# A DeltaNet layer joined to a feed-forward block: the query-key product taken into the product of the keys with the state

## The chip, the cores and the metric

The kernel runs on one core of a Trainium2 chip. The metric is the device time of one execution in microseconds (us). Three runs of the kernel before gave 632.78, 633.17 and 633.45 us; their median, 633.17 us, is the time before. One further execution was recorded by the hardware profiler. In the profile, PE is the matrix engine (TensorE), PEld its weight loads, DVE the vector engine, ACT the scalar engine, POOL the GpSimd engine and SP the queue that issues most of the transfers. All data is float32.

## The reference: what is computed

There are 4 batches of 8 heads, 768 tokens and head size 48. Each of the 32 sequences keeps a 48 x 48 state. A token first reads the state with its query, and then corrects it with its key and value. The 8 heads of a token, 384 numbers, then go through a layer of 2048 with an exact GELU and back to 384.

```python
def _attn_ref(q, k, v, beta):
    k_n = k / (np.linalg.norm(k, axis=-1, keepdims=True) + 1e-06)
    state = np.zeros((B, H, D, D))
    for t in range(S):
        y[:, :, t] = einsum('bhd,bhde->bhe', q[:, :, t], state)
        v_old = einsum('bhde,bhd->bhe', state, k_n[:, :, t])
        state = state + beta * einsum('bhd,bhe->bhde', k_n[:, :, t], v - v_old)
def _moe_ref(x, w_in, w_out):          # x: 3072 x 384, the y of all tokens
    h = x @ w_in
    return (0.5 * h * (1.0 + erf(h / sqrt(2)))) @ w_out
```

## The kernel before, in words

**Chunks.** The 768 steps are cut into 12 chunks (c = 0 to 11) of C = 64 tokens. Inside a chunk the steps are turned into matrix products. A *unit* is a chunk of two batches with all 8 heads; `u.a` (0 or 1) tells which two, so every chunk has two units. The partitions hold two halves of 64 (`HALF`): for K, V and the results the half p is the batch. The state `St` (line 187) lies as 128 partitions x (unit, 2, 4, 48): the partition half r is the parity of the head, and the place in the third dimension is `p ^ r`, with p the batch and j (0 to 3) the pair of heads.

**The small matrix products.** The array of TensorE is used as four quadrants of 64 x 64. `QUADS` (line 48) names them in the order in which they are issued: (r, p) is the half of the partitions read, and the half written. One product over a unit is 4 pairs of heads x 4 quadrants = 16 matmuls; a float32 matmul shows as two records in the trace, so 32 records per unit.

**One chunk of the recurrence**, from chunk 2 on:

1. `against_state` (line 709): for each unit the transposed keys `Kt` times the state, 16 matmuls with 48 moving columns, and the transposed queries `Qt` times the state, 16 more. Both go into one PSUM tile `psK`.
2. `subtract` (line 731): DVE forms `psK - V` (L738) for each unit, then multiplies by the factor gm (L744); this is the right side of the solve. ACT copies the query part to `y` (L739).
3. `solve` (line 751): the triangular inverse `Zf` times that right side (psU, L762). `solved` copies the result U with ACT (L770, L772).
4. `queries` (line 447, through `products`, line 416): Q K^T of both units, 32 matmuls (64 records) with 64 moving columns, line 423. DVE multiplies the result by the causal mask into `P` (L459); for chunks from 4 on this is put off to a moment of its own (`cover`).
5. `outputs`: P times U (psY, L792), K^T times U for the new state (L803), then DVE adds to the state (L808) and forms the chunk's output (L818, with y).
6. `turns`: the output is transposed for the feed-forward block (L854).

Transposes of K and Q: for chunks 0 to 3 by TensorE (`transposed`, L402, copied by L403); from chunk 4 on by DVE in blocks of 32 x 32 (`turned_k`, L408, and `turned_q`, L413) out of `Kb` and `Qb`, which `load_blocks` (L138) fills by 8 transfers per unit. `Qt` is a tile with two buffers.

**PSUM.** The products of the recurrence share the pool tag `dn` (line 72), two buffers of two banks each, taken in turn. A product that starts a new `dn` tile waits until the tile before the last one has been read.

**The rest of TensorE's stream** is the feed-forward block: from chunk 4 on two chunks are worked at a time (`ffn_steps`), by a scheme with seven products for eight, in full-array matmuls of 256 columns (L994) and 192 columns (L928). They are tied in a fixed row (`behind`, line 935). Its sums and GELUs are on DVE and ACT (L1022 to L1107). Where a pair of heads' inverse is found, POOL eliminates row by row (L523, L525), after POOL's power (L360) and DVE's factors (L307 to L311).

**The order.** All steps carry a time `t` in units of a chunk of the feed-forward block, and `emit` writes them in that order. DVE runs in exactly that order (`manual_schedule`). The order on the other engines is chosen by the framework's scheduler when the kernel is built, save that `together` (line 610) ties the TensorE instructions of its steps into one unbroken row, and `keep` holds some ACT instructions in the order written. SP's transfers are issued in order, and a transfer whose target is still in use holds up those behind it. Each even chunk c from 4 on has its plan in the loop `for w in range(4, NC, 2)`: `begins` are the moments of join 1, join 2, then `against_state`, `solve`, `outputs`, `turns` of chunk w, and the last four those of chunk w+1.

Q K^T stands, before, at: chunk 2 alone (t = 2.725); chunks 3, 7, 9, 11 tied behind their solve; chunks 6, 8, 10 tied behind join 1; chunks 4 and 5 in steps of their own.

Of the kernel before, what the change touches and what calls it, by code (L numbers as in the profile page):

```python
# [8 lines left out]
F32 = mybir.dt.float32  # L9
# [5 lines left out]
ALU = mybir.AluOpType  # L15
# [4 lines left out]
def kernel(  # L20
# [82 lines left out]
    for c in range(NC):  # L103
        for a in range(NA):
# [6 lines left out]
            else:  # L111
                u.Kn, u.Kp = Kp[2 + a], Kp[(4 if c % 2 == 0 else 0) + a]
                u.Kb, u.Qb = blocks_of[a], blocks_of[2 + a]

    def load(c):
        for a in range(NA):
            u = tiles[c, a]
            fetch_in(u.Kp[:, :, 0:D], k, u)
            fetch_in(u.Qp[:, :, 0:D], q, u)

    def load_k(c, name):

# [176 lines left out]
    def heads(ap):  # L299
        return ap.rearrange("q (j r) d -> q r j d", r=2)  # L300
# [87 lines left out]
    def transposed(u, part=(0, 1)):  # L388
        for x in part:
            if x == 0:  # L390
                dst = u.Kt = wk.tile([128, 2, NP, C], F32, tag="Kt", name="Kt", bufs=6)
            elif u.c == 1:
                dst = u.Qt = su.tile([128, 2, NP, C], F32, tag="Qt1", name="Qt1")
            else:
                dst = u.Qt = wk.tile([128, 2, NP, C], F32, tag="Qt", name="Qt")
            if x and u.c == 3:
                psT = dn("psT")[:, 0].rearrange("q (j n) -> q j n", n=128)
            else:
                psT = sq("psT", NP, 128)
            flat = (Qp[2 + u.a] if u.c == 3 and x == 0 else (u.Kp, u.Qp)[x]).rearrange("q h d -> q (h d)")  # L400
            for j in range(NP):
                nc.tensor.transpose(psT[:, j, :], flat[:, j * 128:(j + 1) * 128], ident)  # L402
            nc.scalar.copy(dst.rearrange("q p j n -> q j p n"),  # L403
                           psT.rearrange("q j (p n) -> q j p n", p=2))
# [41 lines left out]
    def queries(us):  # L446
        c = us[0].c
        psP = products(us, 1)
        if c not in Ps:
            Ps[c] = (su if c == 1 else wk).tile([128, NA * H, C], F32, tag=f"P{c == 1}", name="P",  # L450
                                                bufs=1)
        for u in us:
            u.P = Ps[c][:, u.a * H:(u.a + 1) * H]
        dst = heads(Ps[c][:, us[0].a * H:(us[-1].a + 1) * H])
        if c < 2:
            nc.scalar.copy(dst, psP)
        else:
            both = mask.unsqueeze(1).to_broadcast([128, len(us) * H, C])
            masks[c] = lambda: nc.vector.tensor_tensor(dst, psP, heads(both), op=ALU.mult)  # L459
            if c < 4:  # L460
                masks[c]()

    masks = {}

    def cover(c):
        masks[c]()

    def masked(u, engine=nc.gpsimd):
        engine.tensor_tensor(u.P, u.P, mask_h, op=ALU.mult)
# [241 lines left out]
    def against_state(us):  # L711

        for u in us:
            u.W = u.V
            u.y = None
            if u.c == 0:
                nc.gpsimd.tensor_tensor(u.W, u.V,
                                        ng[:, u.a].unsqueeze(2).to_broadcast([128, H, D]),
                                        op=ALU.mult)
                continue  # L720
            u.psK = dn("psK")[:, :, 0:2 * NP * D].rearrange("q r (x j d) -> q x r j d", x=2, d=D)
            for x in range(2):
                for j in range(NP):
                    for r, p in QUADS:
                        rows = slice(r * C, r * C + D)
                        to = HALF[p ^ (j % 2)] if x and u.c > 1 else HALF[p]
                        nc.tensor.matmul(u.psK[to, x, r, j, :], lhsT=(u.Qt if x else u.Kt)[rows, p, j, :],  # L727
                                         rhs=St[rows, u.a, p ^ r, j, :], start=True, stop=True)
        if us[0].c > 2:
            subtract(us)  # L730

    def subtract(us):

        for u in us:
            if u.c == 0:
                continue
            u.y = wk.tile([128, H, D], F32, tag="y", name="y")
            nc.vector.tensor_tensor(heads(u.W), u.psK[:, 0], heads(u.V), op=ALU.subtract)  # L738
            nc.scalar.copy(heads(u.y), u.psK[:, 1])  # L739
        for u in us:  # L740
            if u.c == 0:
                continue
            gm = gms[u.c // 2][:, u.t]
            nc.vector.tensor_tensor(u.W, u.W, gm.unsqueeze(2).to_broadcast([128, H, D]),  # L744
                                    op=ALU.mult)

    def quarters(ap):

        return ap.rearrange("q p (k r d) -> q p k r d", r=2, d=D)

    def solve(us, copies=(nc.scalar.copy, nc.scalar.copy)):
        psU = dn("psU")
        for u in us:
            zf = Zf[(u.c // 2) % 2]
# [442 lines left out]
                sum_of_squares(*x)  # L1197
        queries([u])
    for a in range(NA):
        fetch_in(tiles[2, a].Qp[:, :, 0:D], q, tiles[2, a])  # L1200
    for a in range(NA):
        fetch_in(Qp[2 + a][:, :, 0:D], k, tiles[3, a])
    for n in range(2, NS):
# [66 lines left out]
    def state_at(c, *times, first=(), second=(), last=()):  # L1270

        steps = state_steps(c, first, second, last)
        if len(times) > len(steps):
# [11 lines left out]
    plan += [at(1.48, 1.8, sums), at(1.81, 1.811, [(1.0, fn, c) for c in (2, 3) for fn in (norms, prep)]), at(1.9, 1.905, [(1.0, finish_both)]), at(2.725, 2.726, [(1.0, queries, third)]),  # L1285
             at(1.31, 1.311, [(1.0, together, (against_state, first[NA:]))]),
             at(1.325, 1.326, [(1.0, subtract, first[NA:])]),
             at(1.42, 1.421, [(1.0, together, (solve, first[NA:], ()))]),
# [23 lines left out]
    for c in range(4, NC):  # L1312
# [15 lines left out]
    def query(c):  # L1328
        return [(queries, [tiles[c, a] for a in range(NA)])]

    def spread(name, n, *times):
        return [at(t, t + 0.001, [(1.0, copy_out, name, n)]) for t in times]
# [15 lines left out]
    for c in (2, 3, *range(4, NC, 2)):  # L1348
# [8 lines left out]
        else:  # L1357
# [7 lines left out]
             state_at(3, 3.367, 3.59, 3.72, 3.93, second=query(3))]  # L1365
    plan += rows_of(2, 3, ((1, 0.112, 0.113), (2, 0.14, 0.18), (31, 0.2, 0.6),
                           (1, 1.15, 1.151), (1, 1.155, 1.156), (1, 1.157, 1.158)))
    for w in range(4, NC, 2):
        more_to_come = w + 2 < NC
        if w == 4:  # L1370
            begins = 0.21, 0.29, 0.36, 0.45, 0.53, 0.63, 0.7, 0.77, 0.86, 0.93
# [11 lines left out]
        if w == 4:  # L1383
            one = [tiles[w, a] for a in range(NA)]
            plan += [[(t, (together, step)) for t, step in (
                (begins[0], (join_both, 2, 0)), (w + 0.235, *query(w)), (begins[1], (join_both, 2, 1)),
                (w + 0.335, *gram(w + 2)), (begins[2], (against_state, one[:1])),
                (w + 0.405, (against_state, one[1:])), (w + 0.49, *gram(w + 3)))],
                     state_at(w, None, *begins[3:6], last=query(w + 1))]
        else:  # L1390
            plan += [at(begins[0], begins[0] + 0.001, [(1.0, together, (join_both, w // 2, 0), *query(w))]),
                     at(begins[1], begins[1] + 0.001, [(1.0, together, (join_both, w // 2, 1), *gram(w + 2))]),
                     state_at(w, *begins[2:6], second=gram(w + 3))]
        plan += [state_at(w + 1, *begins[6:], second=() if w == 4 else query(w + 1))]
        plan += [at(w + t, w + t + 0.001, [(1.0, take, i % 2)]) for i, t in enumerate(takes)]
        plan += [at(t, t + 0.001, [(1.0, cover, c)])
                 for t, c in ((w + 0.24 if w == 4 else w - 0.261, w), (w + 0.64 if w == 4 else begins[7] + 0.03, w + 1))]
# [39 lines left out]
```

## Time and profile before

| what | value |
|---|---|
| median of 3 runs | 633.17 us (632.78 to 633.45) |
| the profiled execution | 634.08 us; its span 632.4 us; mean granted TensorE clock 0.982 |
| PE, PEld, DVE, ACT, POOL busy | 611.8, 546.6, 428.4, 241.5, 210.2 us |
| psG from Qt and Kt (L423) | 768 records in all, 640 of them in chunks 2 to 11; 48x64 |
| psK from Kt, and from Qt (L727) | 704 records each; 48x48 |
| mask P (L459) | 10 on DVE, 1214 ns each, 128x1024 |
| L738, L744 on DVE | 22 each, 552 and 576 ns, 128x384 |
| y (L739) on ACT | 22, 479 ns each |
| Q's transpose on DVE (L413) | 16, 687 ns each |
| transfers of Q's blocks on SP (L138) | 128; some 0.45 us each on the queue, 2.2 to 2.3 us to landing |

Busy time by stage, in us of the profiled execution:

| stretch | length | PE | DVE | ACT | POOL |
|---|---|---|---|---|---|
| 0 to 60 | 60 | 46.33 | 52.02 | 33.83 | 21.61 |
| 60 to 140 | 80 | 78.36 | 73.61 | 49.12 | 4.18 |
| 140 to 200 | 60 | 59.91 | 44.98 | 28.08 | 28.08 |
| 200 to 250 | 50 | 49.00 | 38.71 | 20.14 | 23.80 |
| 250 to 340 | 90 | 90.00 | 60.56 | 31.72 | 43.61 |
| 340 to 432 | 92 | 91.97 | 60.52 | 31.34 | 46.04 |
| 432 to 524 | 92 | 92.00 | 58.72 | 24.95 | 42.90 |
| 524 to 632 | 108 | 104.23 | 39.32 | 22.32 | 0.00 |

How to read it: the end of a matmul in the trace is modelled and successive matmuls overlap, so the time that a block takes from the stream is read from its start to the start of the next block, not from its busy time. Chunks 2 to 5 run at about 140, 184, 234 and 259 us; from there a pair of chunks takes about 92 us, with the even chunk's `against_state` at about 317, 409 and 500 us, and the odd one's 24 us later.

### The profile page before, as it was taken

To read this page: it belongs to the slowest core of one execution; us is meant where nothing else is said; L and a number is where in the kernel's file an instruction comes from. 1 tells how busy PE (TensorE), PEld (TensorE's weight loads), DVE (VectorE), ACT (ScalarE), POOL (GpSimd) and SP (SyncE) were. 2 spreads that over 40 slices of the span, in tenths; PEclk is the share of its full clock that TensorE was granted. 3 is DMA by queue.
4 is the path that set the end of the run, shared out by engine and by line. 5 is a ranking of instruction groups with operands and counts; after the bars stand their busy time and mean duration, and the time that the engine had idled before them with its cause. 6 is when DMAs were issued, how large, how long until landed. Compare 5 with 4: busy or idle time off the path is not lost.

```text
span 632.4 us, 20834 instructions
## 1 busy us (share of the span) xinstructions
PE 611.8 (97%) x8998; PEld 546.6 (86%) x8998; DVE 428.4 (68%) x783; ACT 241.5 (38%) x546; POOL 210.2 (33%) x316
## 2 busy tenths in 40 slices
PE   6779999999999999999999999999999999999997
PEld 5668886676899998998899998899998899988997
DVE  6999989999866597564868654967645955432532
ACT  3576876625452246224442024442024322044200
POOL 4045001000389721797112688113687100000000
PEclk9975999999999999999999999999999999999999
DMA  9794766102434433533024523025121001010011
GB/s 133 172 286 131 160 143 173 25 1 43 75 46 72 70 60 42 90 77 43 11 39 70 98 51 46 7 40 90 28 50 22 8 2 27 2 26 1 0 26 26
DMA packets 158428, 39.71 MB, mean 63 GB/s; under 512 B 150016, under 2 KB 153216, under 8 KB 158336
## 3 DMA queue, kind: packets, MB, share of 16 engines
q1 hardware_dynamic: 155664, 37.34, 31.0%
q10 hardware_dynamic: 2672, 1.03, 0.8%
q8 instruction: 71, 1.16, 0.8%
q14 instruction: 21, 0.17, 0.1%
HBM read 33.62 MB, written 4.72 MB: 61 GB/s over the span
## 4 chain that ended last, share of the span: by engine, by line
PE 76%; DVE 15%; DMA 3%; issue 2%; SPq 2%; ACT 1%; DVEq 0%
PE psX L928 12%; PE psY L994 10%; PE psY L928 9%; PE psX L994 8%; PE psV L994 5%; PE psZ L994 5%; PE psV L928 4%; PE psZ L928 4%; PE psK L727 3%; DVE Nu L525 3%; DVE tmp L523 3%; PE psO L895 3%; PE psG L423 2%; PE psH L877 2%; PE psY L792 2%
## 5 line engine op out<-in xcount | busy, mean ns | idle before, releaser
L360 POOL TENSOR_TENSOR n<-n,half 128x16 f32<-128x16 f32 x10 | 30.0, 3001 | 186.5 <-DVE n L358 136.6
L525 POOL TENSOR_TENSOR Nu<-Nu,tmp 128x30 f32<-128x30 f32 (+14 forms) x120 | 65.2, 543 | 9.0
L523 POOL TENSOR_TENSOR tmp<-Nu 128x30 f32<-128x30 f32 (+14 forms) x120 | 62.0, 517 | 9.3
L994 PE MATMUL psX<-xT,w_in_sb 128*128 128x256 f32 (+1 forms) x288 | 62.5, 346 | 0.0
L928 PE MATMUL psX<-w_out_sb,G 128*128 128x192 f32 x320 | 56.4, 329 | 0.0
L928 PEld LDWEIGHTS psX<-w_out_sb,G 128*128 128x128 f32 x320 | 52.1, 190 | 0.7
L994 PEld LDWEIGHTS psX<-xT,w_in_sb 128*128 128x128 f32 x288 | 47.9, 191 | 5.2
L877 PE MATMUL psH<-xT,w_in_sb 128*128 128x256 f32 x192 | 46.1, 396 | 0.8 <-ACT G L883 0.6
L877 PEld LDWEIGHTS psH<-xT,w_in_sb 128*128 128x128 f32 x192 | 37.1, 197 | 8.3 <-ACT G L883 1.9
L895 PE MATMUL psO<-w_out_sb,G 128*128 128x384 f32 x128 | 43.9, 490 | 0.0
L994 PE MATMUL psY<-xT,w_in_sb 128*128 128x256 f32 (+1 forms) x192 | 41.6, 346 | 0.0
L1022 DVE TENSOR_TENSOR psY<-psY,pu 128x512 f32<-128x512 f32 x20 | 14.0, 700 | 39.6 <-PE psY L994 38.8
L977 ACT COPY xT<-psX 128x768 f32<-128x768 f32 x9 | 7.2, 799 | 86.2 <-PE psX L854 86.2
L977 ACT COPY pu<-psZ 128x512 f32<-128x512 f32 x40 | 23.5, 587 | 35.2 <-PE psZ L994 35.2
L895 PEld LDWEIGHTS psO<-w_out_sb,G 128*128 128x128 f32 x128 | 23.6, 190 | 14.0
L994 PEld LDWEIGHTS psY<-xT,w_in_sb 128*128 128x128 f32 x192 | 32.1, 191 | 3.5
L977 ACT ACTIVATE G<-G 128x512 f32<-128x512 f32 x40 | 25.2, 630 | 19.2 <-DVE G L1030 19.1
L977 ACT ACTIVATE G<-psY 128x512 f32<-128x512 f32 x20 | 11.9, 597 | 44.7 <-PE psY L994 44.7
L1030 DVE TENSOR_TENSOR G<-psY,pu 128x512 f32<-128x512 f32 x20 | 13.7, 684 | 21.8 <-PE psY L994 21.7
L928 PE MATMUL psZ<-T,pu 128*128 128x192 f32 x160 | 28.3, 329 | 0.1
L928 PE MATMUL psY<-T,G 128*128 128x192 f32 x160 | 28.2, 329 | 0.0
L928 PE MATMUL psY<-w_out_sb,G 128*128 128x192 f32 x160 | 28.1, 329 | 0.0
(198 smaller groups left out, 1372.7 us busy)
## 6 DMA issues: line engine op xcount, KB each, us to landing
Kp<-in_k_dram SPq DMA_DIRECT2D x76, 96.0 KB, 3.4
w_out_sb<-in_moe_w_in_dram SPq DMA_DIRECT2D x24, 256.0 KB, 4.8
w_raw<-in_moe_w_out_dram SPq DMA_DIRECT2D x16, 384.0 KB, 5.0
V<-in_v_dram SPq DMA_DIRECT2D x48, 96.0 KB, 3.2
out_dram<-o_sb SPq DMA_DIRECT2D x40, 96.0 KB, 2.2
Qp<-in_k_dram SPq DMA_DIRECT2D x64, 32.0 KB, 2.4
Qp<-in_q_dram SPq DMA_DIRECT2D x64, 32.0 KB, 2.3
Qp<-in_q_dram SPq DMA_DIRECT2D x16, 96.0 KB, 4.6
```

Of the source, the lines that this page charges most:

```text
L360: nc.gpsimd.tensor_tensor(flat, flat, half, op=ALU.pow)
L423: nc.tensor.matmul(psG[HALF[p], r, i * NP + j, :], lhsT=u.Kt[rows, p, j, :], rhs=(u.Qt if x else u.Kt)[rows, p, j, :], start=True, stop=True)
L523: rows_on.tensor_tensor(tmp, nu[:, j + 1:, j:j + 1].to_broadcast([128, n, j]), nu[:, j:j + 1, 0:j].to_broadcast([128, n, j]), op=ALU.mult)
L525: rows_on.tensor_tensor(nu[:, j + 1:, 0:j], nu[:, j + 1:, 0:j], tmp, op=ALU.add)
L727: nc.tensor.matmul(u.psK[to, x, r, j, :], lhsT=(u.Qt if x else u.Kt)[rows, p, j, :], rhs=St[rows, u.a, p ^ r, j, :], start=True, stop=True)
L877: nc.tensor.matmul(psH, lhsT=w_in_sb[:, f // 2, m, f % 2 * 128:(f % 2 + 1) * 128], rhs=xTs[c][:, m, :], start=(m == 0), stop=(m == NM - 1))
L895: nc.tensor.matmul(u.psO, lhsT=G[:, u.a, f, :], rhs=w_out_sb[:, f, :], start=(f == 0), stop=(f == NF - 1))
L928: nc.tensor.matmul(ps_, lhsT=lhs[:, f, :], rhs=rhs[:, f, :], start=first and f == 0, stop=f == FH - 1, skip_group_check=not first)
L977: i = fn(*args, **kw)
L994: nc.tensor.matmul(ps_[:, i], lhsT=lhs[:, f // 2, f % 2 * 128:(f % 2 + 1) * 128], rhs=rhs, start=first and i == 0, stop=True, skip_group_c ...
L1022: nc.vector.tensor_tensor(L1["Y1"], L1["Y1"], L1["pu"][:, 0], op=ALU.add)
L1030: nc.vector.tensor_tensor(half(1, 1), shaped(L1["Y1"]), shaped(L1["pu"][:, 0]), op=ALU.add)
```

## The change

From chunk 2 on, the transposed queries are written beside the state, into one tile `SQ` of 48 + 64 = 112 columns per place. The product of the keys with it gives K times the state and K Q^T in the same 16 matmuls per unit; `queries` is no longer called for these chunks, and the mask into P is done by DVE from `psK` in `subtract`. The queries' product with the state becomes a function of its own, `against_queries`, placed at the head of `solve`, with a `dn` tile of its own for both units (`psQ`); the copies to y go with it. Since the place of a state in `SQ` is `p ^ r`, the queries of odd heads have to be loaded with the two batches changed over, so the transfers for r = 1 are split by batch (`fetch_q`, `load_blocks`). There is only one place for the transposed queries of a unit, where the tile before had two buffers; the times of `turned_q` for odd chunks are later (chunk 5: 4.57 for 4.4; chunks 7, 9, 11: c - 0.77 for c - 0.93). Chunks 0 and 1 keep their separate product.

```diff
+    def fetch_q(u):
+        rows = slice(u.c * C, (u.c + 1) * C)
+        for p in range(2):
+            for r in range(2):
+                nc.sync.dma_start(out=u.Qp[HALF[p ^ r], r::2, 0:D],
+                                  in_=q[2 * u.a + p, r::2, rows, :].rearrange("h t d -> t h d"))
...
                         to = slice((2 * r + e) * HB, (2 * r + e + 1) * HB)
+                        if r and name == "Qb":
+                            for p in range(2):
+                                n0_ = (2 * a + p) * H
+                                nc.sync.dma_start(
+                                    out=dst[to, 1 - p, :, h, 0:w],
+                                    in_=src[n0_ + 1:n0_ + H:2, rows,
+                                            e * HB:e * HB + w].rearrange("n t d -> t n d"))
+                            continue
...
-    St = cpool.tile([128, NA, 2, NP, D], F32)
+    SQ = cpool.tile([128, NA, 2, NP, D + C], F32, name="SQ")
+    St = SQ[:, :, :, :, 0:D]
...
     def turned_q(u):
-        u.Qt = wk.tile([128, 2, NP, C], F32, tag="Qt", name="Qt")
-        nc.vector.transpose(u.Qt.rearrange("q p j n -> q (p j n)"),
-                            u.Qb.rearrange("q p j h n -> q (p j h n)"))
+        u.Qt = SQ[:, u.a, :, :, D:]
+        nc.vector.transpose(u.Qt.rearrange("q p j n -> q (p j) n"),
+                            u.Qb.rearrange("q p j h n -> q (p j) (h n)"))
...
     def against_state(us):
...
-            u.psK = dn("psK")[:, :, 0:2 * NP * D].rearrange("q r (x j d) -> q x r j d", x=2, d=D)
-            for x in range(2):
-                for j in range(NP):
-                    for r, p in QUADS:
-                        rows = slice(r * C, r * C + D)
-                        to = HALF[p ^ (j % 2)] if x and u.c > 1 else HALF[p]
-                        nc.tensor.matmul(u.psK[to, x, r, j, :], lhsT=(u.Qt if x else u.Kt)[rows, p, j, :],
-                                         rhs=St[rows, u.a, p ^ r, j, :], start=True, stop=True)
+            w = D if u.c == 1 else D + C
+            psK = dn("psK")
+            u.psK = psK[:, :, 0:NP * w].rearrange("q r (j d) -> q r j d", d=w)
+            for j in range(NP):
+                for r, p in QUADS:
+                    rows = slice(r * C, r * C + D)
+                    nc.tensor.matmul(u.psK[HALF[p], r, j, :], lhsT=u.Kt[rows, p, j, :],
+                                     rhs=SQ[rows, u.a, p ^ r, j, 0:w], start=True, stop=True)
...
+    def against_queries(us):
+        c = us[0].c
+        if c > 1:
+            psQ = dn("psQ")[:, :, 0:NA * NP * D].rearrange("q r (a j d) -> q a r j d", a=NA, d=D)
+        for u in us:
+            if c > 1:
+                u.psQ = psQ[:, u.a]
+            for j in range(NP):
+                for r, p in QUADS:
+                    rows = slice(r * C, r * C + D)
+                    to, x = (HALF[p ^ (j % 2)], p ^ r) if c > 1 else (HALF[p], p)
+                    nc.tensor.matmul(u.psQ[to, r, j, :], lhsT=u.Qt[rows, x, j, :],
+                                     rhs=St[rows, u.a, p ^ r, j, :], start=True, stop=True)
+        for u in us:
+            u.y = wk.tile([128, H, D], F32, tag="y", name="y")
+            nc.scalar.copy(heads(u.y), u.psQ)
...
     def subtract(us):
...
         for u in us:
-            nc.vector.tensor_tensor(heads(u.W), u.psK[:, 0], heads(u.V), op=ALU.subtract)
-            nc.scalar.copy(heads(u.y), u.psK[:, 1])
+            if c > 0:
+                nc.vector.tensor_tensor(heads(u.W), u.psK[:, :, :, 0:D], heads(u.V), op=ALU.subtract)
+            if c > 1:
+                u.P = Ps[c][:, u.a * H:(u.a + 1) * H]
+                nc.vector.tensor_tensor(heads(u.P), u.psK[:, :, :, D:], heads(mask_h), op=ALU.mult)
...
     def solve(us, copies=(nc.scalar.copy, nc.scalar.copy)):
+        if us[0].c > 1:
+            against_queries(us)
         psU = dn("psU")
...
-        t = {4: 3.88, 5: 4.4}.get(c, c - (0.47 if even else 0.93))
+        t = {4: 3.88, 5: 4.57}.get(c, c - (0.47 if even else 0.77))
         plan += [at(t, t + 0.01, [(1.0, turned_q, u) for u in us])]
```

The steps `query(c)` and `cover` are taken out of the plan, and one time of the plan for chunk 5 (0.7) becomes 0.67. In the order that the built kernel has, chunk 5's `against_state` then stands directly behind chunk 4's `turns`, one L928 product earlier than before.

More of the change, by code (lines that the diff above doesn't have):

```diff
@@ L118, in load @@
             fetch_in(u.Kp[:, :, 0:D], k, u)
-            fetch_in(u.Qp[:, :, 0:D], q, u)
+            fetch_q(u)
     def load_k(c, name):
@@ L394, in transposed @@
             else:
-                dst = u.Qt = wk.tile([128, 2, NP, C], F32, tag="Qt", name="Qt")
+                dst = u.Qt = SQ[:, u.a, :, :, D:]
             if x and u.c == 3:
@@ L449, in queries @@
         if c not in Ps:
-            Ps[c] = (su if c == 1 else wk).tile([128, NA * H, C], F32, tag=f"P{c == 1}", name="P",
+            Ps[c] = (su if c == 1 else wk).tile([128, NA * H, C], F32, tag=f"P{c == 1:d}", name="P",
                                                 bufs=1)
@@ L453, in queries @@
             u.P = Ps[c][:, u.a * H:(u.a + 1) * H]
[L454 to L466, printed above, removed]
+        nc.scalar.copy(heads(Ps[c][:, us[0].a * H:(us[-1].a + 1) * H]), psP)
     def masked(u, engine=nc.gpsimd):
@@ new lines, in against_state @@
+            psK = dn("psK")
[5 more added lines that the diff above has]
+                                     rhs=SQ[rows, u.a, p ^ r, j, 0:w], start=True, stop=True)
+            if u.c == 1:
+                u.psQ = psK[:, :, NP * D:2 * NP * D].rearrange("q r (j d) -> q r j d", d=D)
+                against_queries([u])
@@ L732, in subtract @@
     def subtract(us):
+        c = us[0].c
+        if c > 1 and c not in Ps:
+            Ps[c] = wk.tile([128, NA * H, C], F32, tag="P0", name="P", bufs=1)
         for u in us:
[L735 to L738, printed above, removed]
-            nc.scalar.copy(heads(u.y), u.psK[:, 1])
-        for u in us:
[L741 to L745, printed above, removed]
+            if c > 0:
[3 more added lines that the diff above has]
+                nc.vector.tensor_tensor(heads(u.P), u.psK[:, :, :, D:], heads(mask_h), op=ALU.mult)
@@ L747, in quarters @@
+        for u in us:
+            if c > 0:
+                gm = gms[c // 2][:, u.t]
+                nc.vector.tensor_tensor(u.W, u.W, gm.unsqueeze(2).to_broadcast([128, H, D]),
+                                        op=ALU.mult)
     def quarters(ap):
@@ L1199 @@
     for a in range(NA):
-        fetch_in(tiles[2, a].Qp[:, :, 0:D], q, tiles[2, a])
+        fetch_q(tiles[2, a])
     for a in range(NA):
@@ L1284 @@
     sums = [(1.0, sum_of_squares, tiles[3, a], h) for a in range(NA) for h in range(H)]
-    plan += [at(1.48, 1.8, sums), at(1.81, 1.811, [(1.0, fn, c) for c in (2, 3) for fn in (norms, prep)]), at(1.9, 1.905, [(1.0, finish_both)]), at(2.725, 2.726, [(1.0, queries, third)]),
+    plan += [at(1.48, 1.8, sums), at(1.81, 1.811, [(1.0, fn, c) for c in (2, 3) for fn in (norms, prep)]), at(1.9, 1.905, [(1.0, finish_both)]),
              at(1.31, 1.311, [(1.0, together, (against_state, first[NA:]))]),
@@ L1326, in gram @@
         return [(grams, [tiles[c, a] for a in range(NA)])] if c < NC else []
-    def query(c):
-        return [(queries, [tiles[c, a] for a in range(NA)])]
     def spread(name, n, *times):
@@ L1364 @@
              at(3.11, 3.111, [(1.0, finish, 4)]),
-             state_at(3, 3.367, 3.59, 3.72, 3.93, second=query(3))]
+             state_at(3, 3.367, 3.59, 3.72, 3.93)]
     plan += rows_of(2, 3, ((1, 0.112, 0.113), (2, 0.14, 0.18), (31, 0.2, 0.6),
@@ L1370 @@
         if w == 4:
-            begins = 0.21, 0.29, 0.36, 0.45, 0.53, 0.63, 0.7, 0.77, 0.86, 0.93
+            begins = 0.21, 0.29, 0.36, 0.45, 0.53, 0.63, 0.67, 0.77, 0.86, 0.93
             takes = 0.212, 0.214, 0.292, 0.294
@@ L1385 @@
             plan += [[(t, (together, step)) for t, step in (
-                (begins[0], (join_both, 2, 0)), (w + 0.235, *query(w)), (begins[1], (join_both, 2, 1)),
+                (begins[0], (join_both, 2, 0)), (begins[1], (join_both, 2, 1)),
                 (w + 0.335, *gram(w + 2)), (begins[2], (against_state, one[:1])),
                 (w + 0.405, (against_state, one[1:])), (w + 0.49, *gram(w + 3)))],
-                     state_at(w, None, *begins[3:6], last=query(w + 1))]
+                     state_at(w, None, *begins[3:6])]
         else:
-            plan += [at(begins[0], begins[0] + 0.001, [(1.0, together, (join_both, w // 2, 0), *query(w))]),
+            plan += [at(begins[0], begins[0] + 0.001, [(1.0, together, (join_both, w // 2, 0))]),
                      at(begins[1], begins[1] + 0.001, [(1.0, together, (join_both, w // 2, 1), *gram(w + 2))]),
                      state_at(w, *begins[2:6], second=gram(w + 3))]
-        plan += [state_at(w + 1, *begins[6:], second=() if w == 4 else query(w + 1))]
+        plan += [state_at(w + 1, *begins[6:], second=())]
         plan += [at(w + t, w + t + 0.001, [(1.0, take, i % 2)]) for i, t in enumerate(takes)]
-        plan += [at(t, t + 0.001, [(1.0, cover, c)])
-                 for t, c in ((w + 0.24 if w == 4 else w - 0.261, w), (w + 0.64 if w == 4 else begins[7] + 0.03, w + 1))]
         if more_to_come:
```

## The prediction

> **What bounds the kernel now.** I read the page's busy times and slices, then the stages, then the chain, then the instructions in order of time around one chunk. One part of the page, three of its lines:
>
> ```profile
> PE 611.8 (97%) x8998; PEld 546.6 (86%) x8998; DVE 428.4 (68%) x783; ACT 241.5 (38%) x546; POOL 210.2 (33%) x316
> ...
> PE   6779999999999999999999999999999999999997
> ...
> PE 76%; DVE 15%; DMA 3%; issue 2%; SPq 2%; ACT 1%; DVEq 0%
> ```
>
> TensorE is busy in every slice from about 50 us on, and the chain is TensorE for 76%. From 250 to 524 us its busy time equals the stretch: work taken off its stream there shortens the run, if nothing that it waits for gets late. The stream around chunk 9's recurrence (start, length, line, shapes, records):
>
> ```profile
> 432.31 0.68 PE L727 MATMUL psK<-St,Kt 48*64 48x48 f32 x32
> 432.81 0.65 PE L727 MATMUL psK<-St,Qt 48*64 48x48 f32 x32
> 433.27 0.65 PE L727 MATMUL psK<-St,Kt 48*64 48x48 f32 x32
> 433.74 0.65 PE L727 MATMUL psK<-St,Qt 48*64 48x48 f32 x32
> 434.32 2.87 PE L928 MATMUL psY<-w_out_sb,G 128*128 128x192 f32 x16
> 437.02 2.76 PE L928 MATMUL psV<-w_out_sb,G 128*128 128x192 f32 x16
> 439.71 1.15 PE L762 MATMUL psU<-V,Zf 64*64 64x48 f32 x64
> 440.68 1.13 PE L423 MATMUL psG<-Qt,Kt 48*64 48x64 f32 x64
> 441.74 2.87 PE L928 MATMUL psX<-w_out_sb,G 128*128 128x192 f32 x16
> ```
>
> Read the starts, not the lengths (they overlap). A float32 matmul leaves two records. 32 records of 48 columns take 433.27-432.81 = 0.467 us, 58.4 ns for four; the four quadrants of the array run at once. Starts of the 64-column block, counted in narrow windows, also come four in 58.4 ns. So 48 and 64 columns cost the same: a floor per instruction, which a longer moving operand could use up. The full array has no such floor: L994's 128x256 blocks start every 863 ns for four records, 215.8 each; 128x192 162.5; 128x128 109.2. These three lie on 0.833 ns per column plus 2.5 ns. A visit to small tiles costs 0.04 us more on entry and 0.11 on leaving, and the product ahead of it 0.1.
>
> VectorE between this chunk's product with the state and its solve:
>
> ```profile
> 433.54 0.56 DVE L738 TENSOR_TENSOR V<-psK,V 128x384 f32<-128x384 f32 x1 [0.61 <-PE psK L727]
> 434.47 0.56 DVE L738 TENSOR_TENSOR V<-psK,V 128x384 f32<-128x384 f32 x1 [0.38 <-PE psK L727]
> 434.94 1.02 DVE L744 TENSOR_TENSOR V<-V,gm 128x384 f32<-128x384 f32 x2
> ...
> 445.25 1.22 DVE L459 TENSOR_TENSOR P<-psG,mask 128x1024 f32<-128x1024 f32 x1
> ```
>
> The right side is ready at 435.96, the solve (psU) starts at 439.71: 3.7 us of cover. The mask L459 comes off the path, after the solve.
>
> **The change, part by part.** 1. Removed: the block of Q with K in chunks 2 to 11, 64 records, 16 groups x 58.4 = 0.93 us, with its ends 1.06 behind psU (440.68 to 441.74) and 1.09 behind a join (psJ). Behind psU the leaving cost of 0.11 passes to psU, so 0.95 goes.
> 2. Longer: K with the state, 16 groups of 48 columns per chunk (0.93) become 16 of 112. No row has 112 columns in a quadrant. Low end: 58.4 ns a group, if the floor covered 112 too. High end: the two quadrants that read the same partitions take turns, 2 x 95.8 = 191.6. I take 0.833 x 112 + 2.5 = 95.8: the full array never beats that, and the 64-column group (55.8 by the same line) already runs all four at 58.4, so the rows nearest in shape show no turns. 16 x 95.8 = 1.53, so +0.60.
> 3. Moved: Q with the state (0.93) leaves the burst and goes in front of the solve, +0.95 there and -0.93 here, with its PSUM buffer in the place of the removed block's.
> The work per chunk is then, behind a join (6, 8, 10; 2 alike): -1.09 + 0.60 + 0.02 = -0.47; behind psU (3, 7, 9, 11): -0.95 + 0.62 = -0.33; chunks 4 and 5, where the block stood alone between products and also cost its neighbour 0.1 or twice 0.1: -0.67 and -0.57. Sum: 4 x 0.47 + 4 x 0.33 + 1.24 = 4.44 us off the stream.
> 4. The mask moves between L738 and L744: two of 128x512 per chunk. Bounds by row: half of L459's 1214 ns = 0.61, or L1022's 128x512 with PSUM on both sides, 0.70. I take 0.65. VectorE in sum: +20 x 0.65 - 12.1 = +0.9 us, at 68%. On the path +1.3 us per chunk against 3.7 us of cover (odd) and, in even chunks, L744 ending at 412.74 against a solve at 416.82. Cover: two to five feed-forward products. Without it 1.3 x 10 = 13 us. Queued behind: L1042 and the L358 sums. L1042 would end at 414.6 at the latest, before ScalarE's Gelu on it (414.82). L358 feeds POOL's 2.91 us power and then L307, which VectorE waits at: some 1.3 us later, repaid by the missing L459 (1.22) right behind.
> 5. Q's transpose now writes the one place beside the state, so it must follow the last read of the old Q. In chunks 7, 9, 11 it comes behind L1066 (ends 429.92), +1.29 = 431.2, while psK wants 432.31: 1.1 us of slack. In chunk 5 the built order puts psK one product earlier and the transposes behind L493 (254.30): 255.6, against a wanted start of 254.8 with the first half ready at 255.0. Cost 0.25; bounds 0 to 0.8.
> 6. The y copies (479 ns each) go from L738's wait to just ahead of the solve's copies. In chunks 6 and 8 the gram block behind psU takes psQ's buffer and must wait for both: ScalarE has L1078 (0.32) and two squares (0.94) queued when psQ starts, so y ends some 0.1 + 1.26 + 0.94 - 0.1 = 2.2 us after that; the block is ready after psQ and psU, 0.04 + 0.93 + 0.97 = 1.95. Cost 0.25 twice; bounds 0 to 0.5 each.
> 7. Gains on waits: in chunk 3 psZ and psX of L928 start at 196.03 and 199.09 and psY at 202.04, 3.06 and 2.95 apart instead of 2.70, with L408 late because it waited until 195.70 for the removed block, and psY waited 0.19 on L459. In chunk 4 psK waited at 234.31, 0.56 in all, with L459 (228.68) in front on a VectorE that had no idle time. Together some -1.1, bounds 0 to -1.5. Against it: the built order now interleaves chunk 4's second join with psZ, two more changes of tile size, +0.25; chunk 2's solve, L744 later by 1.3, +0.1.
> Items 5 to 7 cancel: 0.25 + 0.5 + 0.35 - 1.1 = 0.0 (from -1.5 to +2.2).
> 8. DMAs: Q's blocks of r=1 and Q of chunks 2, 3 are split: 8 x 8 + 8 = 72 more issues at about 0.45 us on SP. SP had four sends of chunk 8 at 438.26 behind the 16 Q issues at 421.36; now 24 that wait for the transpose at 431: sends near 441 to 444, landed by 447, and o_sb is next written behind psY at 454. Ahead of the first weights four more issues: +2 us on loads landing near 36 to 38, decoded from about 49. Both hidden; uncovered the first would cost some 5 us once per pair of chunks.
>
> Sum: 634.08 (the profiled run: span 632.4 and 1.7 around it) - 4.4 = 629.6; the median of the runs shown, 633.17, is 0.9 lower: **628.7**. By the bounds of 5 to 7: 627.2 to 630.9.
>
> **The rivals.** (a) Long columns overlap worse. By the line above one 64-column record would need 55.8 ns and one of 48 columns 42.5; four of either take 58.4, so the array does 3.8 and 2.9 records' work at once. With the lesser of the two, a group of 112 takes 4 x 95.8 / 2.9 = 132 ns: 160 groups x 36 = +5.8, **634.5, slightly slower**. For it: no row has more than 64 columns in a quadrant; against: the longer of the two rows overlaps better, not worse. The Trainium skill, "TensorE: Matmul & The Clock Gate", Part 3 ("Measured speedup vs the span model"), speaks for it: four row tiles with 512 columns gained 3.07 of 4, which as an estimate by that page would be 125 ns a group and 633.4 us here; this trace's 3.8 at 64 columns is better than that, and no run here shows longer ones. (b) Quadrants on the same partitions take turns beyond 64 columns: 160 x 95.8 = +15.3, **644, slower**. It decides from 124 ns a group, where the 4.4 is used up. Against: at 64 columns turns would already give 107. (c) The mask ahead of the solve makes VectorE or ScalarE late: 1.3 us in the four chunks 2 to 5, where VectorE is fullest (38.7 of 50 us in 200:250), gives +5.2: 633.9; in all chunks 641. For it: no idle time at 225 to 241; against: 2.4 us of cover left elsewhere, and L459 gone. (d) Q's single place stalls psK in 5, 7, 9, 11 by 0.5: 630.7. Against: the 1.1 us above.
>
> **How the numbers follow.** Forecast as summed 0.70, (d) 0.08, (c) 0.11 (0.02 faster, 0.05 same, 0.04 slower), (a) 0.05 (0.02 same, 0.03 slower, as the overlap is nearer 3.1 or 2.9 of 4), (b) 0.06. 0.2% is 1.3 us, about what a measurement of this kernel tells from none. Faster 0.80, same 0.07, slower 0.13. The range for 8 in 10: low 626.8, just under the gains of 7 in full; high 632.6, which takes in (d) and the smaller half of (c) and leaves (a) and (b) out.
>
> **What would show it.** psK's 32 records of one unit spaced near 24 ns, 0.77 us; 14.6 would mean a floor, 31 no gain, 48 turns. No psG from Qt after chunk 1. The next product's start minus psK's first near 1.7 us (2.01 before). psU starting straight behind psQ, without a wait for the right side (L744's product); a gap there is (c). A psK waiting on the Q transpose is (d). A gram block waiting on y in chunks 6 and 8 shows item 6. I am wrong if psK's spacing is off, or if TensorE's busy share falls below 97%.

## The result, and the profile after

The changed kernel is slower: 639.33 us median (637.69 to 642.88, four executions) against 633.31 us for the kernel before (632.78 to 634.15). The ratio is 1.0101, 95% interval 1.0056 to 1.0147. The forecast was 628.7 us and faster.

The profiled execution took 637.69 us (span 636.0), 3.61 us more than that of before. Its busy times and slices, and the chain:

```profile
PE 608.2 (96%) x8358; PEld 542.4 (85%) x8358; DVE 426.8 (67%) x793; ACT 240.7 (38%) x546; POOL 209.4 (33%) x316
...
PE   6779999999999999999999998999998999999997
...
PEclk9986999999999999999999999899999999999999
...
PE 70%; DVE 14%; POOL 5%; DMA 4%; issue 3%; ACT 2%; SPq 2%; DVEq 0%; POOLq 0%
```

TensorE's busy time fell by 3.6 us, yet its share fell as well. Two slices that were full are so no longer (near 390 and 490 us), and behind the first of them the granted clock drops to 8 tenths. POOL, which had no place in the chain before, now has 5% of it.

The stream around chunk 9's recurrence, in order of time (start, length, line, shapes, records):

```profile
434.63 1.76 PE L731 MATMUL psK<-SQ,Kt 48*64 48x112 f32 x64
...
441.73 1.15 PE L751 MATMUL psQ<-SQ 48*64 48x48 f32 x64
442.69 1.11 PE L791 MATMUL psU<-V,Zf 64*64 64x48 f32 x64
443.74 2.87 PE L957 MATMUL psX<-w_out_sb,G 128*128 128x192 f32 x16
```

From psK to the product behind psU this took 443.74 - 434.63 = 9.11 us; before, 432.31 to 441.74, it was 9.43. The 0.32 us less are what was forecast for such a chunk (0.33), and psK is 1.70 us, also as forecast. Here the change does what it was expected to do. What takes it back is in the table of TensorE's waits (total, times, longest):

```profile
PE psJ L650 <- DVE XM L538: 5.2, 2, 3.0
...
PE psK L731 <- DVE SQ L429: 0.5, 1, 0.5
PE psZ L1023 <- DVE TX L988: 0.4, 1, 0.4
```

The first is new: the first join of the chunks 8 and 10 (psJ, the product that brings the parts of the inverse together) waits 2.96 and 2.24 us for the transposed rows of the inverse (XM). Before, psJ of chunk 8 started at 395.16 and no wait was listed for it. Followed back, the chain of the changed kernel reads (start, length, what):

```profile
353.41 3.87 DMA V<-in_v_dram
...
357.44 0.83 POOL V L401
358.27 0.22 POOL tmp L527
...
362.98 0.79 POOL V L401
...
393.63 0.26 POOL Nu L529
393.91 2.05 DVE XM L538
396.00 1.16 PE psJ L650 x64
```

A transfer of V lands at 357.28. POOL scales that V (L401), then works through the rows of the elimination (L527 and L529), with a second scaling in their midst, until 393.9; then come XM and the join. POOL before and after at this place:

```profile
354.66 2.37 POOL L508 TENSOR_TENSOR Nu<-Nu,XM 128x1024 f32<-128x1024 f32 x1 [4.84 <-DVE Nu L503]
357.10 0.25 POOL L523 TENSOR_TENSOR tmp<-Nu 128x30 f32<-128x30 f32 x1
```

```profile
351.43 2.37 POOL L512 TENSOR_TENSOR Nu<-Nu,XM 128x1024 f32<-128x1024 f32 x1 [3.23 <-DVE Nu L507]
357.44 0.83 POOL L401 TENSOR_TENSOR V<-V,n 128x384 f32<-128x384 f32 x1 [3.64 <-DMA V<-in_v_dram]
358.23 0.25 POOL L527 TENSOR_TENSOR tmp<-Nu 128x30 f32<-128x30 f32 x1
```

The product ahead of the rows is 3.2 us earlier than before, the first row 1.1 us later: between them POOL stood for 3.64 us at V. In the end XM is ready 0.84 us later than before (395.95 against 395.11), while TensorE comes there 2.1 us earlier; the wait is the two together. And V is late because of SP's queue. Before, and then after (start, length of the run of issues, what, how many):

```profile
328.09 8.62 SPq L138 DMA_DIRECT2D Qp<-in_q_dram  x16
336.81 2.66 SPq L100 DMA_DIRECT2D V<-in_v_dram  x4
```

```profile
335.99 1.06 SPq L153 DMA_DIRECT2D Qp<-in_q_dram  x2
...
346.08 0.43 SPq L153 DMA_DIRECT2D Qp<-in_q_dram  x1
346.61 3.42 SPq L918 DMA_DIRECT2D out_dram<-o_sb  x4
350.07 0.59 SPq L153 DMA_DIRECT2D Qp<-in_q_dram  x1
350.71 1.89 SPq L148 DMA_DIRECT2D Qp<-in_q_dram  x4
352.70 3.91 SPq L100 DMA_DIRECT2D V<-in_v_dram  x4
```

The blocks of Q for chunk 8 may be sent only when chunk 7's transpose has read the old ones. That transpose is later in the changed plan (it ends at 335.62, before at 326.14), so the first send is 7.9 us later. The built order lets sends of K, which before stood behind V, go ahead in the meantime; they end at 335.89, at about the moment at which the transpose does. There are 24 sends of Q instead of 16, and four sends of results fall among them. V stands behind all that: 352.70 instead of 336.81, although TensorE is 2.1 us ahead.

The second wait has the same pattern. POOL's product ahead of the rows of chunk 10 (L512) stands behind a scaling that waited 5.28 us for V:

```profile
451.43 0.83 POOL L401 TENSOR_TENSOR V<-V,n 128x384 f32<-128x384 f32 x1 [5.28 <-DMA V<-in_v_dram]
```

Behind the first wait TensorE also ran slower:

```profile
396.00 1.16 PE L650 MATMUL psJ<-XM,G 32*64 32x64 f32 x64 [2.96 <-DVE XM L538]
397.09 1.90 PE L1023 MATMUL psV<-xT,w_in_sb 128*128 128x256 f32 x4
398.78 1.91 PE L1023 MATMUL psY<-TX,w_in_sb 128*128 128x256 f32 x4
400.49 1.15 PE L1023 MATMUL psY<-xT,w_in_sb 128*128 128x256 f32 x4
```

The starts of these blocks are 1.69 and 1.71 us apart; equal blocks in the version without the wait (below) are 0.97 and 0.86 apart. Against that version the slow blocks cost 1.68 us (the starts lie 3.12 us apart at psJ, 4.80 from 401.47 on). So 2.96 + 2.24 + 1.68 = 6.88 us were added, and 637.69 - 634.08 - 6.88 = -3.27 us is what the rest of the change brought in this execution. The longer ones of the four were not profiled; what they lost beyond this is not shown.

### The profile page after: what moved, and what is told of

Same layout as the page of the kernel before. It is cut to its first block, busy times and chain, and to the rows that moved or that the text cites. A ratio compares the mean times of both kernels' runs of the same rounds, so it can differ in the third digit from the quotient of the medians.

```text
span 636.0 us, 19679 instructions
## 1 busy us (share of the span) xinstructions
PE 608.2 (96%) x8358; PEld 542.4 (85%) x8358; DVE 426.8 (67%) x793; ACT 240.7 (38%) x546; POOL 209.4 (33%) x316
## 3 DMA queue, kind: packets, MB, share of 16 engines
HBM read 33.62 MB, written 4.72 MB: 60 GB/s over the span
## 4 chain that ended last, share of the span: by engine, by line
PE 70%; DVE 14%; POOL 5%; DMA 4%; issue 3%; ACT 2%; SPq 2%; DVEq 0%; POOLq 0%
PE psX L957 11%; PE psY L1023 9%; PE psY L957 8%; PE psX L1023 6%; PE psV L1023 5%; PE psZ L1023 4%; PE psZ L957 4%; PE psV L957 4%; PE psG L439 3%; PE psK L731 3%; POOL Nu L529 3%; POOL tmp L527 2%; PE psH L906 2%; PE psT L418 2%; PE psU L791 2%
## 5 line engine op out<-in xcount | busy, mean ns | idle before, releaser
L376 POOL TENSOR_TENSOR n<-n,half 128x16 f32<-128x16 f32 x10 | 30.2, 3022 | 185.1 <-DVE n L374 135.3
L529 POOL TENSOR_TENSOR Nu<-Nu,tmp 128x30 f32<-128x30 f32 (+14 forms) x120 | 65.6, 546 | 9.0
L527 POOL TENSOR_TENSOR tmp<-Nu 128x30 f32<-128x30 f32 (+14 forms) x120 | 60.9, 507 | 9.2
L837 DVE TENSOR_TENSOR SQ<-SQ,psY 128x384 f32<-128x384 f32 x21 | 11.6, 554 | 30.8 <-PE psY L832 30.5
```

Source lines behind the costliest of these rows:

```text
L376: nc.gpsimd.tensor_tensor(flat, flat, half, op=ALU.pow)
L527: rows_on.tensor_tensor(tmp, nu[:, j + 1:, j:j + 1].to_broadcast([128, n, j]), nu[:, j:j + 1, 0:j].to_broadcast([128, n, j]), op=ALU.mult)
L529: rows_on.tensor_tensor(nu[:, j + 1:, 0:j], nu[:, j + 1:, 0:j], tmp, op=ALU.add)
```

## The experiments

Theory T: V's transfers, held behind the sends of Q, hold up POOL, whose rows had no time to spare, and that is the whole loss. Rival R: the rows were made late by the mask ahead of the solve, which pushes back the sums that POOL's power waits for (L376 started at 440.53 instead of 436.96, 1.6 us more than the 2.0 by which TensorE itself was late there). Four runs were made on one chip against the same runs of before (633.55 us median), then four more (before: 633.82).

**V sent first.**

```diff
-        t = c - (1.35 if c % 2 and c > 5 else 1.0)
+        t = c - (1.35 if c % 2 and c > 5 else 1.405 if c > 6 else 1.0)
         plan += [at(t, t + 0.01, [(1.0, load_v, c)])]
```

> The changed kernel with one time of its plan altered: V of the even chunks 8 and 10 is sent for just ahead of the blocks of Q (at c - 1.405 instead of c - 1.0). Theory T: in the changed kernel the transfers of V stand behind 24 sends of Q that wait for the later transpose (V landed at 357.28 us), POOL scales V ahead of the rows of the elimination, so the rows start late and join 1 of chunks 8 and 10 waits 2.96 and 2.24 us, and 1.7 us more go at a lower TensorE clock behind the first wait. Then all of it goes: 637.7 - 6.9 = 630.8 us (629.5 to 632). Rival R: the rows had no cover, and it is the mask ahead of the solve, which delays the sums and POOL's power, that makes them late; then the two waits stay and the time stays at 637 to 640.

Measured: 629.46 us median (629.40 to 630.59), ratio to before 0.9931 (0.9908 to 0.9953). SP's issues of V, and the windows at the first join of chunk 8 (length; busy us and instructions of PE, PEld, DVE, ACT, POOL; granted clock; DMA share and GB/s):

```profile
335.59 2.65 SPq L100 DMA_DIRECT2D V<-in_v_dram  x4
```

```profile
393.00:398.00 5.00, 5.00 (x83) 4.47 (x84) 4.82 (x9) 1.37 (x3) 2.06 (x2) 1.00 0.24 30
398.00:403.00 5.00, 5.00 (x142) 4.28 (x141) 4.34 (x9) 2.57 (x5) 0.00 (x0) 1.00 0.07 10
```

V is sent 17 us sooner than in the changed kernel, TensorE is busy throughout, both waits at psJ are gone and the clock stays at 1.00; in the changed kernel the same two windows have a clock of 0.93 and 0.73. The mask is where it was. T holds, and R falls. The profiled executions of the two are 7.10 us apart, and the two waits with the lower clock (6.88) make up nearly all of it. The medians, taken on two occasions, are 9.9 apart; where the rest of that went is not shown.

**POOL in the order of the plan.**

```diff
-    with tc.manual_schedule(engines={mybir.EngineType.DVE}):
+    with tc.manual_schedule(engines={mybir.EngineType.DVE, mybir.EngineType.Pool}):
         emit(*plan)
```

> The changed kernel with POOL's instructions also in the order of the plan, so that V of the even chunks is scaled behind the rows instead of ahead of them or among them; SP's order, and V's late landing, stay. Theory T: the rows no longer stand behind V's transfer, both waits at join 1 go, 630.8 us (629.5 to 632.5). If V's late landing hurts in another way (SP's queue as a whole), or by rival R (the mask makes the rows late), the waits stay: 636 to 640.

Measured: 630.36 us (629.14 to 631.10), ratio 0.9942 (0.9923 to 0.9961); no wait at psJ in chunk 8 or 10. V is as late as ever (sent at 355.29), but the first row starts at 354.07, straight behind the product ahead of it:

```profile
351.63 2.36 POOL L512 TENSOR_TENSOR Nu<-Nu,XM 128x1024 f32<-128x1024 f32 x1 [3.24 <-DVE Nu L507]
354.07 0.25 POOL L527 TENSOR_TENSOR tmp<-Nu 128x30 f32<-128x30 f32 x1
```

So a late V by itself costs nothing; it costs because of what stands behind it on POOL. Either repair is enough.

**The blocks of Q unsplit** in chunks 8 to 11.

```diff
-                        if r and name == "Qb":
+                        if r and name == "Qb" and c < 8:
```

> The changed kernel with the blocks of Q of chunks 8 to 11 sent for unsplit, as before: 16 sends instead of 24 per chunk. The odd heads of these chunks then get the other batch's queries, so those outputs differ from the reference; the amount of work is the same. Theory T: V is sent for 8 x 0.48 = 3.9 us sooner; the rows of chunk 8 start about 0.8 us sooner and lose the scaling in their midst (0.83), those of chunk 10 about 3.8: the wait of 2.96 falls to about 1.3, that of 2.24 goes, time about 633 (631.5 to 635). Rival R: no change, 637 to 640. If the split alone were the whole cause: 630.8.

Measured: 630.99 us (628.52 to 632.50), ratio 0.9958 (0.9943 to 0.9974); the profiled execution took 632.50. One wait is left, 2.48 us at chunk 8, the other is gone. The pattern is the one expected; the wait left is longer than the 1.3 said (both scalings now stand ahead of the rows), and the median 2 us better, outside the range that was stated. So the split is a good part of the cause in the changed kernel, but not all of it.

**The kernel before with Q's new way in, and nothing else:** the later transpose, and the split sends for chunks 8 to 11.

```diff
-        t = {4: 3.88, 5: 4.4}.get(c, c - (0.47 if even else 0.93))
+        t = {4: 3.88, 5: 4.4}.get(c, c - (0.47 if even else 0.77))
...
+                        if r and name == "Qb" and c > 7:
+                            for p in range(2):
+                                n0_ = (2 * a + p) * H
+                                nc.sync.dma_start(
+                                    out=dst[to, p, :, h, 0:w],
+                                    in_=src[n0_ + 1:n0_ + H:2, rows,
+                                            e * HB:e * HB + w].rearrange("n t d -> t n d"))
+                            continue
```

> The kernel before, with only the two changes to Q's way in: the transpose of Q of the odd chunks from 7 on at c - 0.77 instead of c - 0.93, and the blocks of the odd heads of chunks 8 to 11 sent for in two halves (24 sends for 16). No mask is moved, the products are those of before. Theory T: V lands at about 359 and 451, POOL takes the first scaling ahead of the product in front of the rows, the rows start some 6 and 4.6 us later, and as they had no cover, join 1 of chunks 8 and 10 waits about that long: 634 + 10.6 and some us at a lower clock, 645 (639 to 650). Rival R (the mask): no change, 633 to 634.5.

Measured: 649.53 us (645.17 to 651.10), ratio 1.0237 (1.0194 to 1.0279). Its waits, POOL at chunk 8 and the windows behind the first wait:

```profile
PE psJ L654 <- DVE XM L542: 10.5, 2, 5.7
```

```profile
358.93 0.83 POOL L393 TENSOR_TENSOR V<-V,n 128x384 f32<-128x384 f32 x1 [11.05 <-DMA V<-in_v_dram]
```

```profile
398.00:403.00 5.00, 3.17 (x112) 3.06 (x116) 4.96 (x5) 0.63 (x1) 2.02 (x3) 0.50 0.07 9
403.00:408.00 5.00, 5.00 (x38) 4.07 (x32) 4.42 (x9) 0.00 (x0) 1.30 (x2) 0.50 0.01 3
```

The waits are 5.74 and 4.72 us, where 6 and 4.6 were expected. Behind each the granted clock is 0.50 for some 7.6 us; by the starts of equal products against the trace of before, the difference grows from 4.67 to 8.42 us behind the first and from 13.21 to 17.02 behind the second, 3.8 us each. The old products with the new way in for Q make the whole loss, and more than it: three of V's four sends go even later here (from 355.88 instead of 352.70), and both of V's scalings stand ahead of the rows.

**Each half alone in the kernel before.** The edits are the first and the second part of the diff above.

> The kernel before with the later transpose of Q alone (odd chunks from 7 on, c - 0.77 for c - 0.93), the sends of Q unsplit. Theory T: Q's 16 sends of chunk 8 still wait for the transpose and V stands behind them, but is sent for some 4.5 us sooner than with the split; POOL's rows start 1 to 2.5 us late in chunks 8 and 10 and join 1 waits as long: 634 + 3 = 637 (635 to 640). Were the later transpose harmless by itself: 633 to 634.5. Were it the whole cause: as with both, 645 to 650.

Measured: 636.11 us (634.26 to 638.70), ratio 1.0046 (1.0025 to 1.0066). In the profile one wait, 1.88 us at chunk 8, and 1.6 us at a lower clock behind it. None at chunk 10, where one had been expected.

> The kernel before with the split sends of Q in chunks 8 to 11 alone (24 for 16), the transpose at its old moment. Theory T: Q's sends start as early as before (328 us), V is sent for 3.9 us later but still lands ahead of POOL's first scaling of it (347 us): no wait, 633 to 634.5. Were the split the cause by itself: above 637.

Measured: 634.16 us (632.17 to 635.48), ratio 1.0003 (0.9987 to 1.0018), no wait. Here the sends of Q start at 328.24, those of V at 342.13, and POOL scales V at 346.75 and 348.13, before the product ahead of the rows could start (354.85).

So the two halves don't add up: the later transpose alone costs 2.3 us, the split alone nothing that can be told, both together 16. It goes by when the sends of V for chunk 8 begin (with the later transpose, and with both, the last three of the four; the first goes ahead of Q there): 336.81 before; 342.13 with the split, no wait; 349.23 with the later transpose, 1.88 us; 355.88 with both, 5.74. The first 5 us at least are free; beyond that the wait grows with the delay, chunk 10 comes in too, and the lower clock adds to both.

**Other widths of the moving operand,** on the version with V first. The state's tile gets 16 more columns of zeros.

```diff
-            w = D if u.c == 1 else D + C
+            w = D if u.c == 1 else {6: 64, 7: 80, 8: 96, 9: 128}.get(u.c, D + C)
...
-                nc.vector.tensor_tensor(heads(u.P), u.psK[:, :, :, D:], heads(mask_h), op=ALU.mult)
+                x_ = min(D, u.psK.shape[-1] - C)
+                nc.vector.tensor_tensor(heads(u.P), u.psK[:, :, :, x_:x_ + C], heads(mask_h), op=ALU.mult)
```

> The version with V sent first, with another moving width of K's product with the state in four chunks: 64 columns in chunk 6, 80 in 7, 96 in 8, 128 in 9 (16 columns of zeros behind Q), 112 in 10 and 11. In chunks 6 to 8 a part of the columns of Q is left out and the mask reads the last 64 columns that there are, so their outputs differ from the reference; the lengths of the instructions are what is looked at. By the line of the full array (0.833 ns a column + 2.5, four quadrants at once, not under 58.4 a group) a record takes 14.6, 17.3, 20.6, 24.0 and 27.3 ns at 64, 80, 96, 112 and 128 columns. By rival (a), 2.9 of 4 at once, 80 would be 23.8, 96 28, 128 37.6; by rival (b), turns, 34, 41 and 55.

One execution was made, 629.19 us, and its trace is read for the lengths alone:

```profile
311.62 1.16 PE L732 MATMUL psK<-SQ,Kt 48*64 48x64 f32 x64
...
335.66 1.34 PE L732 MATMUL psK<-SQ,Kt 48*64 48x80 f32 x64
...
403.80 1.55 PE L732 MATMUL psK<-SQ,Kt 48*64 48x96 f32 x64
...
428.23 1.98 PE L732 MATMUL psK<-SQ,Kt 48*64 48x128 f32 x64
```

From start to the next product's start the blocks take 1.091, 1.268, 1.481, 1.694 (112 columns) and 1.907 us; inside, a record takes 15.0, 17.6, 20.8, 23.9 and 27.1 ns. From 80 columns up, each 16 columns cost 0.213 us, which for 64 records is 0.208 ns a column, a quarter of the 0.833 of the full array: four quadrants at once, with no loss up to 128 columns. Rivals (a) and (b) of the prediction are out. At 64 the floor (14.6) and the line (13.9) almost meet.

**The product of chunk 5 back in its place,** with V first.

```diff
-            begins = 0.21, 0.29, 0.36, 0.45, 0.53, 0.63, 0.67, 0.77, 0.86, 0.93
+            begins = 0.21, 0.29, 0.36, 0.45, 0.53, 0.63, 0.7, 0.77, 0.86, 0.93
```

> The version with V sent first, and the product of K with the state of chunk 5 one feed-forward product later again (0.7 in the plan for 0.67). Its first record then no longer waits 0.47 us for the transpose of Q. Theory: 629.5 - 0.5 = 629.0 (628.3 to 629.6), if the right side of chunk 5, one product of 2.6 us closer to its solve, is still ready; if not, 629.5 to 632.

Measured: 629.99 us (629.16 to 630.01), ratio 0.9945 (0.9928 to 0.9962). The wait of 0.47 us is gone from the trace and psU of chunk 5 doesn't wait; the median lies above the 628.3 to 629.6 expected, and the medians of this and of V first cannot be told apart.

## Why the prediction was wrong, point by point

The step that failed is item 8, the 72 more sends. The prediction followed the queue to the sends of results ("sends near 441 to 444, landed by 447, and o_sb is next written behind psY at 454") and called it hidden. It did not follow it to the loads of V, which stand in the same queue behind the same 24 sends, and from there to POOL, where the built order puts V's scaling ahead of the rows. And it gave the later transpose no effect beyond that, though it holds the sends back by 7.9 us. Nor did it look at how much time the rows had. In the trace of before:

```profile
393.00 2.11 DVE L534 STREAM_TRANSPOSE XM<-Nu 128x1024 f32<-128x1024 f32 x1 [0.58 <-POOL Nu L525]
```

```profile
394.11 1.03 PE L994 MATMUL psV<-xT,Sw 128*128 128x256 f32 x4
395.16 1.16 PE L646 MATMUL psJ<-XM,G 32*64 32x64 f32 x64
```

XM ended at 395.11, 0.05 us ahead of the join that needs it, and the join came 1.05 us behind the block ahead of it, where it comes 0.96 behind in the version with V first. So it was already held up by 0.1 us: there was no cover left. What it named as the price of a lost cover, "some 5 us once per pair of chunks", came close to the mark for one that is lost in full (5.74 and 4.72); the changed kernel lost 2.96 and 2.24, and the lower clock was no term of it. None of the four rivals was this one. Of its two signs of being wrong, TensorE's busy share below 97% came (96%); psK's spacing was as said.

The other steps, by differences of equal products' starts between the traces of before and of the version with V first, where the new waits are out of the way:

- 1 to 3, the products: the block behind the join of chunks 6, 8 and 10 gave 1.09 to 1.19 (in chunk 8 the 0.1 us that its join waited before is in it), behind psU 0.98; psK's group of four costs 95.8 ns (64 records of 23.95); psQ 0.97. Right, to a tenth at most.
- 4, the mask: 0.68 us for 128x512 (0.65 taken). The right side of chunk 8's solve ends at 415.3, that of chunk 9's at 439.5; their solves start at 418.9 and 442.7 (all four in the changed kernel). Hidden, as said. The power was 1.6 us later (1.3 said).
- 5: no wait for Q's transpose in chunks 7, 9 and 11; 0.47 in chunk 5 (0.25 taken, bounds 0 to 0.8). Rival (d), a wait in all four, came in one of them.
- 6: psU takes 1.17 us ahead of the gram block in chunks 6 and 8, 0.21 more than before (0.25 taken).
- 7: psZ and psX of chunk 3 now take 2.70 and 2.70 (0.61 less), the waits of chunk 4's psK fell from 0.56 to 0.16: about 1.0 of the 1.1 said. The interleaved join cost 0.44 (0.25): from psX behind psY to the next psY it now takes 3.51 us instead of 3.07.
- Not in it at all: by 158 us TensorE was 1.1 us ahead of before, 0.48 of it from chunk 2, and at 167 only 0.04. psZ waited there 0.90 us for VectorE, which waited at the transpose of chunk 5's keys for their blocks (until 165.92; before, 165.35). A lead that meets a transfer on its old date is worth nothing.

In sum the profiled execution of that version is 630.59, 3.49 us under before, where 4.4 was forecast: 0.5 went with chunk 2's gain, 0.2 in chunk 5, the rest in smaller pieces. One pair of executions does not settle tenths in such a sum: of the three kernels of before with another way in for Q alone, which are equal to it up to there, one is 0.2 us behind it at 238 us, the others 1.0 and 2.0 ahead. By the medians on one chip the gain is 633.55 - 629.46 = 4.1 us. Its median, 629.46 us, lies 0.8 above the forecast of 628.7 and inside its range. The cost of the change was misjudged in one place of SP's queue; its gain was not. That version, and the one with POOL in the order of the plan, beat both kernels.

## What to carry to other kernels

When a change adds issues to a queue, or moves what they wait for, list everything that stands behind them in that queue until the next pause, and follow each of them to the engine that needs it and to what stands behind it there. Look then for the step on that second engine that ends just as its reader starts: where a wait has become zero without being counted as one, there is no cover left. Two delays that cost 2.3 us and nothing alone can be 16 us together, since the cover is used once.

## What the runs showed of the hardware

**The clock behind a wait.** After five of the six waits named here, TensorE came back at half its clock. Waits of 1.88, 2.48 and 2.96 us were each followed by 1.6 to 1.7 us of loss, one of 2.24 us by none; waits of 4.72 and 5.74 us by 3.8 us each, with a granted clock of 0.50 in whole windows of 5 us. So a wait of 2 to 3 us can cost more than half as much again, or nothing. The Trainium skill, "TensorE: Matmul & The Clock Gate", Part 1 ("The HAM clock gate"), describes this: half rate after an idle window of about 3.4 us, full rate after about as long a busy one, in windows that run freely. The half rate agrees (0.50), and so does its length behind the short waits (twice 1.6 to 1.7 us); but waits well under 3.4 us set it off here, and behind the long ones it held for 7.6 us.

**Sending is not free.** Sixteen sends of Q took SP 8.62 us, 0.54 each: most 0.45 us, one 1.09. The Trainium skill, "DMA: Bandwidth & Descriptors" ("Issuing engines are not separate DMA queues"), calls the time to initiate a transfer usually small beside the transfer. For one small block the traces agree: 0.45 us, beside the 2 to 3 us until it lands. But 16 or 24 sends stand one behind the other, and their sum set the date of everything behind them.

**Four quadrants at once lose nothing** between 80 and 128 columns: 27.1 ns a record at 128 columns, against 109.2 for the full array.
